# Earlier turns, smaller banks and moved counts in a fused attention and top-1 expert kernel

## Chip, core and metric

The kernel runs on one core of a Trainium2 chip. The metric is the device time of one execution in microseconds; before the change it is 443.85 us, the median of 3 runs (443.0 to 445.07). The profiled execution took 443.64 us, of which the profile shows a span of 439.6 us from the first to the last instruction.

## What is computed

Two blocks follow each other. The first is a cross attention between the rows `x` of a batch and 32 state rows for each head: the rows read from the states, and the states are rewritten from the rows. The second sends each of the 4352 rows that come out to one of eight experts, by the largest logit, and scales the expert's output by the softmax weight of that logit.

```python
# x: (8, 8, 512, 64)   state: (8, 8, 32, 64)
scores = scale * x @ state.T                 # (B, H, 512, 32)
a = softmax(scores);   xread = a @ state     # (B, H, 512, 64)
scores2 = scale * state @ x.T                # (B, H, 32, 512)
a2 = softmax(scores2); sread = a2 @ x        # (B, H, 32, 64)
rows = concatenate([xread, sread], axis=2)   # -> (8 * 544, 512) after heads are merged
logits = rows @ w_gate                       # (4352, 8)
e = argmax(logits); g = softmax(logits)[e]
out = g * (relu(rows @ w1[e]) @ w2[e])       # w1: (8, 512, 1024)  w2: (8, 1024, 512)
```

## The kernel before

The kernel guesses one expert for each batch (the most frequent one among its `x` rows) and computes all 512 `x` rows of the batch with that expert as dense products. Since `xread = a @ state`, it first forms `G = state @ w1[e]` (names `pG`, `G`), so that the up product is `a @ G` (`ph`, results `hT`). The down product is `hT @ w2[e]` (`py` for batches 0 and 1). For batches 2 to 7 both products are done by halves, with seven products of half-size blocks in place of eight, and sums between them (`pX`, `pD`, `pY`, `pZ`, `pW`). The 256 state rows are sorted by expert and computed in rounds of four groups of 32 rows (`pgh`, `pgy`). Rows that don't fit the guess are computed behind a branch at the end, which is skipped if there are none.

Every engine keeps the order of the program (all operations are recorded through one helper, so nearly all profile lines carry the line L48; the names of the tiles tell them apart). Attention of a batch is cut into steps, and a step is taken at each "slot" between the pieces of the dense products:

```python
def stages(b):
    xt, sx = new_xt(), new_sx()
    turn_x(b, xt, slice(0, 4))            # VectorE turns x in 32x32 blocks, four heads at a time
    turn_x(b, xt, slice(4, 8))
    turn_states(b, gp.tensor_copy)        # stT: VectorE, then a copy by GpSimd
    yield
    states_gates(b)                       # pg: states times gate matrix
    pc = new_pc()
    scores(b, xt, pc, 0)                  # pc: scores of half of the heads
    yield
    scores(b, xt, pc, 1)
    for i in range(4): turn_scores(pc, sx, i)
    less_max(sx, ALL, gp)
    nm = write_max(pc)                    # maximum, and its scaling, by VectorE
    yield
    soft[b] = (sx,) + write_weights(pc, nm)
    exponential(sx, ALL); over_sum(sx, ALL, gp)
    yield
    turn_read(b)                          # aT, and its store to at_dram
    yield
    turn_write(b)                         # pt
    yield
    write_rows(b)                         # pw, xs, four stores to srow, then fetch_batch(b + 3)
    exps, gates = logits_x(b)             # pl, lg, and the choice of each row's expert
    yield
    exps(); xsT = turn_rows(b)            # pxs
    yield
    choose(b); logits_s(b, xsT); gates()  # pr (counts), eb (the batch's expert), pls
```

Batches 0 and 1 have an order of their own, as the kernel has nothing else to do while they start. The first loads are the gate's matrix `wg4` and half of batch 0's states on ScalarE's queue, the other half and `x` on SyncE's. The expert of batch 0 is guessed from the sums of its states (`pss`, `prg`), so that its weights can be loaded at once:

```python
act.dma_start(out=wg4[:], in_=moe_w_gate...)
load_states(0, sp, act); load_x(0, sp)
...
def begin():
    keep_warm(3)                          # products whose result nobody reads ("idle")
    # pss: sums of the states; prg: their logits; most(0, pr): the expert of batch 0
    keep_warm(9)
    turn_states(0, act.copy)
    xt, sx = new_xt(), new_sx()
    turn_x(0, xt, slice(0, 4))
    # loads of w1, x and states of batch 1, wg, w2, batch 2
    turn_x(0, xt, slice(4, 8))
    for g in range(2): scores(0, xt, pc, g)
    turn_scores(pc, sx, 0); less_max(sx, one, dve); exponential(sx, one)
    states_w1(G, w1s[0], stG[:, 0], (0,)) # pG, and two copies 128x512 to G by ScalarE
    ...
    keep_warm(5)
    up(G, aT[0], hT, one, fs=near)        # ph
    ...
    def beside():                         # taken between the products of the last up()
        ...
        yield
        # pre
        scores(1, xt, pc, 1)
        exps, gates = logits_x(0)
        # scores of batch 1 turned, less_max, write_max; stages(2) begins: turns of batch 2
        yield
        exps(); gates(); count(0); turn_write(0)
        exponential(sx, ALL); soft[1] = (sx,) + write_weights(pc, nm)
        over_sum(sx, ALL, dve); turn_read(1)
        yield
    up(G, aT[0], hT, half, beside())
```

Products rotate through four PSUM banks of one pool (`bank`); `pc` has banks of its own. At the end of a batch by halves the last product and the last sum are:

```python
product(pD, lambda f: Sa[:, f], W(1, 1), start=False)   # pD: one bank, two halves of 256
store(yB, 1, 0)
add(yA, pD, yA, 0)                                      # two sums 128x256 on VectorE
(store if b < B - 1 else store_each)(yA, 0, 1)          # the last batch: ACT's and SP's queue
```

After that every engine reads the count of rows that are left, and branches.

Of the kernel before, what the change touches and what calls it, by code (L numbers as in the profile page):

```python
# [20 lines left out]
def kernel(  # L21
# [88 lines left out]
    wg4 = att.tile([128, NDC, E], FP32, name="wg4")  # L110
    act.dma_start(out=wg4[:], in_=moe_w_gate.rearrange("(p c) e -> p c e", c=NDC))
    load_states(0, sp, act)
# [89 lines left out]
    def turn_x(b, xt, h):  # L202
        dve.transpose(xt[:, h].rearrange("p h c u t -> p (h c u t)"),
                      x_nat[b][:, h].rearrange("p h c d -> p (h c d)"))
# [20 lines left out]
    def scores(b, xt, pc, g):  # L225

        for u in range(2):
            for q in range(4):
                for i in range(4):
                    pe.matmul(pc[ts(q, 32), i, ts(g, 128)], lhsT=stT[b][ts(i, 32), 2 * q + g, u ^ (i % 2), :],  # L230
                              rhs=xt[ts(i, 32), 2 * q + g, :, u, :],
                              start=(u == 0), stop=(u == 1), skip_group_check=True)
# [23 lines left out]
    def write_max(pc):  # L256
        nm = att.tile([128, 2], FP32, tag="nm", bufs=2, name="nm")
        dve.tensor_reduce(nm[:], pc[:, :, 0:256].rearrange("p i (g s) -> p g i s", g=2), AX.XY, ALU.max)
        dve.tensor_scalar(nm[:], nm[:], -SCALE, None, ALU.mult)
        return nm  # L260

    def write_weights(pc, nm):

        a2 = att.tile([128, 2, NC, 128], FP32, tag="a2", name="a2")
        s2 = att.tile([128, 2], FP32, tag="s2", bufs=2, name="s2")
        for g in range(2):
            act.activation(a2[:, g].rearrange("p c (i t) -> p i c t", i=4),
                           pc[:, :, ts(g, 128)].rearrange("p i (c t) -> p i c t", c=NC),
                           AF.Exp, bias=nm[:, g:g + 1], scale=SCALE, accum_out=s2[:, g:g + 1])
        return a2, s2  # L270
# [4 lines left out]
    def new_xt():  # L275
        return att.tile([128, H, NC, 2, 32], FP32, tag="xt", bufs=1, name="xt")
# [19 lines left out]
    def write_rows(b):  # L296

        _, _, s2, a2T = soft[b]
        pw = bank("pw")[:, 0:128].rearrange("p (g d) -> p g d", g=2)
        for g in range(2):  # L300
            for c in range(NC):
                for q in range(4):
                    pe.matmul(pw[ts(q, 32), g], lhsT=a2T[:, g, c, ts(q, 32)], rhs=x_nat[b][:, 2 * q + g, c, :],
                              start=(c == 0), stop=(c == NC - 1), skip_group_check=True)
        xs = rows_of[b] = att.tile([128, 2, D], FP32, tag="xs", bufs=2, name="xs")
        for g in range(2):
            act.activation(xs[:, g], pw[:, g], AF.Copy, scale=s2[:, g:g + 1])
        for q in range(4):
            sp.dma_start(out=srow[ts(b % 4, NS), b // 4, ts(q, 128)], in_=xs[ts(q, 32)].rearrange("p g d -> p (g d)"))
        fetch_batch(b + 3)  # L310
# [6 lines left out]
    def turn_read(b, i=ALL):  # L317
        if b not in aT:
            aT[b] = att.tile([128, 4, 2, 128], FP32, tag="aT", bufs=NE, name="aTe")[:]
        dve.transpose(aT[b][:, i].rearrange("p i g s -> p (i g s)"),  # L320
                      soft[b][0][:, i].rearrange("p i b n -> p (i b n)"))
        if i.stop == 4:
            sp.dma_start(out=at_dram[b], in_=aT[b].rearrange("p i g s -> p (i g s)"))
# [11 lines left out]
    def stages(b):  # L335

        xt, sx = new_xt(), new_sx()
        turn_x(b, xt, slice(0, 4))
        turn_x(b, xt, slice(4, 8))
# [27 lines left out]
        logits_s(b, xsT)  # L367
# [10 lines left out]
    def logits_s(b, xsT):  # L378

        pl = bank("pls")[ts(b % 4, 32), 0:E]  # L380
        for q in range(4):
            pe.matmul(pl, lhsT=xsT[:, q, :], rhs=wg[:, q, :], start=(q == 0), stop=(q == 3), skip_group_check=True)
        dve.tensor_copy(out=lgs[ts(b % 4, 32), b // 4], in_=pl)
# [47 lines left out]
    def begin():  # L431
# [14 lines left out]
        keep_warm(9)  # L446
        turn_states(0, act.copy)
        xt, sx = new_xt(), new_sx()
        turn_x(0, xt, slice(0, 4))
# [7 lines left out]
        turn_x(0, xt, slice(4, 8))  # L457
        pc = new_pc()
        for g in range(2):
            scores(0, xt, pc, g)  # L460
# [6 lines left out]
        states_w1(G, w1s[0], stG[:, 0], (0,))  # L467
# [23 lines left out]
        xt, sx = new_xt(), new_sx()  # L491
        turn_x(1, xt, slice(0, 4))
        turn_x(1, xt, slice(4, 8))
# [4 lines left out]
        def beside():  # L498
# [12 lines left out]
            exps, gates = logits_x(0)  # L511
# [5 lines left out]
            early.append(stages(2))  # L517
            next(early[0])
            yield
            exps()  # L520
            gates()
            count(0)
            turn_write(0)
            exponential(sx, ALL)
            soft[1] = (sx,) + write_weights(pc, nm)
            over_sum(sx, ALL, dve)
# [46 lines left out]
    def states_w1(G, w1t, st, halves=(0, 1), bank=bank):  # L573

        for k in halves:
# [5 lines left out]
            for g in range(2):  # L581
                act.copy(G[:, g, ts(k, 512)], pg[g][:])
# [138 lines left out]
    def down_by_halves(b, hT, w2t, insert, between):  # L721
# [23 lines left out]
        def product(to, a, w, start=True, stop=True):  # L745
            for c in range(2):
                for f in range(4):
                    pe.matmul(to[:, c], lhsT=a(f)[:, ts(c, 128)], rhs=w[:, f], start=(start and c == f == 0),
                              stop=(stop and f == 3), skip_group_check=True)
            n[0] += 1  # L750
# [16 lines left out]
        def store_each(y, i, k):  # L767
            for c, q in enumerate((act, sp)):
                no_dep(q.dma_start(out=rows[:, 2 * i + c, ts(k, 256)], in_=y[:, c]))

        def add(y, p, u, i):
            for c in range(2):
                dve.scalar_tensor_tensor(y[:, c], p[:, c], g[2 * i + c], u[:, c], ALU.mult, ALU.add)
# [3 lines left out]
        yA, yB = new_y(), new_y()  # L777
# [4 lines left out]
        pD = new_bank("pD")  # L782
# [30 lines left out]
        add(yA, pD, yA, 0)  # L813
        (store if b < B - 1 else store_each)(yA, 0, 1)
# [175 lines left out]
    def rounds(r0, r1):  # L990
# [11 lines left out]
        for r in range(r0, r1):  # L1002
# [16 lines left out]
            for f in range(0, NFC, 4):  # L1019
# [6 lines left out]
                if r + 1 < r1 or f + 4 < NFC:  # L1026
                    for _ in range(3):
                        yield
# [5 lines left out]
    def first():  # L1034

        write_rows(0)
        yield
# [9 lines left out]
        gates()  # L1047
        yield
# [4 lines left out]
        for b in range(2):  # L1053
            logits_s(b, xsT[b])
# [8 lines left out]
    def attention():  # L1063

        gens, slot = [first()], 0
        while gens:
            b = 2 + slot // 3
            old, new = gens[:], slot % 3 == 0 and b < B
            begun = slot < 6
            if begun:  # L1070
                advance(gens, old[:1])
            if new:
                gens.append(early.pop() if early else stages(b))
                if b > 2:
                    next(gens[-1])
# [12 lines left out]
    def batch(b):  # L1088
# [3 lines left out]
        def between(c):  # L1092
            nonlocal G
            if c == (1 if b else 2) and b + 1 < B:
                G = states_w1(new_G(), w1s[b + 1], stG[:, b + 1])
            yield
            if c == 1 and 0 < b < B - 2:
# [19 lines left out]
        else:  # L1117
            down_by_halves(b, hT, w2s[b], slots, between_products)
# [4 lines left out]
        elif b + 1 < B:  # L1123
            hT = up(G, aT[b + 1], new_hT(), insert=slots, at=(1, 3, 5, 7) if b + 1 < NE else (1, 3, 4, 5, 6, 7))
        if b == 0:
# [14 lines left out]
    for b in range(B):  # L1140
        batch(b)
# [9 lines left out]
    with tc.If(number(rest_i, B * S + NG) > 0, label="rest"):  # L1151
# [3 lines left out]
        with tc.If(number(left_i, B * S) > 0):  # L1155
# [65 lines left out]
            fix.release()  # L1221

# [32 lines left out]
```

## Time and profile before

| | |
|---|---|
| time | 443.85 us (443.0 to 445.07) |
| span in the profile | 439.6 us, TensorE clock granted 0.999 |
| matrix products | 427.4 us busy, 3933 instructions |
| VectorE, ScalarE, GpSimd | 225.3, 127.6 and 153.4 us busy |
| moved by DMA | 110.04 MB, mean 250 GB/s |
| instruction fetches (queue q8) | 32 packets, 0.52 MB |
| load of batch 3's `x`: issue on SyncE's queue | 53.16 us |
| last product `pD` | begins at 430.84 us, takes 3.72 us |

An fp32 product appears as two instructions of TensorE, and its weight load as two more. The busy time of TensorE (PE) is the time in which at least one product instruction is under way; the profiler models the end of a product, so busy does not mean at peak. In a table by stretches of the span, the difference between a stretch and the busy time in it is time in which TensorE had no product. A list of waits gives what ended such a pause: an engine and tile, a transfer, or "issue" where nothing that the profile shows was waited for. In the timeline a line has start, duration, engine, operation, tiles as out<-in, and in brackets the pause ahead of it.

### The profile page before, as it was taken

Reading aid. Unit: us, or ns where it says so; the run is one execution under the profiler, and the core shown is the slowest. Engines: PE = TensorE matmul, PEld = TensorE weight load, DVE = VectorE, ACT = ScalarE, POOL = GpSimd, SP = SyncE. Lnnn points to the kernel's source line nnn. Section 1 sums busy time; section 2 is a strip of 40 time slices with the busy share of each in tenths; the row PEclk is TensorE's granted clock in tenths of the full one; section 3 lists DMA queues with packets and bytes.
Section 4 is the critical chain, followed back from the end, with each engine's and each line's share of the span. In section 5 each row is a group of like instructions: output and inputs, shape, how many; then the busy total and the mean of one; then the engine's idle time right before and its main releaser. Section 6 shows DMA issues by size and latency. Waiting matters only on the chain.

```text
span 439.6 us, 10186 instructions
## 1 busy us (share of the span) xinstructions
PE 427.4 (97%) x3933; PEld 289.9 (66%) x3933; DVE 225.3 (51%) x482; ACT 127.6 (29%) x287; POOL 153.4 (35%) x143
## 2 busy tenths in 40 slices
PE   8899989999999999999999999999999999999995
PEld 7675544555555457786768677776867685768673
DVE  4757784787796657333505261523442370527151
ACT  1544233452353442212311241013240242025100
POOL 2010131322422431573327424534335253644231
PEclk9999999999999999999999999999999999999999
DMA  6990289655493454899999799789947998884211
GB/s 185 338 327 7 88 275 324 188 197 159 134 364 111 146 199 146 273 322 399 382 387 325 287 345 392 260 266 397 386 148 250 400 380 270 298 285 170 95 49 59
DMA packets 64513, 110.04 MB, mean 250 GB/s; under 512 B 12943, under 2 KB 22415, under 8 KB 64464
## 3 DMA queue, kind: packets, MB, share of 16 engines
q1 hardware_dynamic: 60240, 99.99, 65.9%
q0 software_dynamic: 2240, 7.08, 4.2%
q10 hardware_dynamic: 1984, 2.31, 1.5%
q8 instruction: 32, 0.52, 0.5%
q14 instruction: 17, 0.14, 0.1%
HBM read 94.15 MB, written 14.95 MB: 248 GB/s over the span
## 4 chain that ended last, share of the span: by engine, by line
PE 85%; DVE 9%; issue 1%; SPq 1%; DMA 1%; POOL 1%; ACT 1%; POOLq 0%; DVEq 0%
PE ph L48 22%; PE pD L48 10%; PE pX L48 10%; PE py L48 7%; PE pY L48 5%; PE pZ L48 5%; PE pgy L48 5%; PE pgh L48 5%; PE pW L48 5%; PE pG L48 3%; PE pc L48 3%; DVE sx L48 2%; DVE xt L48 2%; PE pt L48 1%; DVE sm L48 1%
## 5 line engine op out<-in xcount | busy, mean ns | idle before, releaser
L48 PE MATMUL py<-w2t,hT 128*128 128x512 f32 x128 | 59.0, 604 | 0.0
L48 DVE TENSOR_TENSOR hT<-ph,hT 128x512 f32<-128x512 f32 x50 | 34.6, 692 | 40.7 <-PE ph L48 40.7
L48 POOL TENSOR_TENSOR Ta<-w2t,Ta 128x1024 f32<-128x1024 f32 x12 | 30.6, 2547 | 46.6 <-PE pD L48 26.7
L48 PE MATMUL pX<-w2t,hT 128*128 128x256 f32 x192 | 43.7, 381 | 0.0
L48 PEld LDWEIGHTS pX<-w2t,hT 128*128 128x128 f32 x192 | 36.2, 190 | 6.4 <-issue 1.7
L48 PEld LDWEIGHTS py<-w2t,hT 128*128 128x128 f32 x128 | 23.0, 189 | 25.6 <-issue 24.9
L48 DVE SCALAR_TENSOR_TENSOR yh<-pY,gw,yh 128x256 f32<-128x256 f32 x24 | 10.0, 477 | 54.3 <-PE pY L48 47.8
L48 ACT ACTIVATE hT<-ph 128x512 f32<-128x512 f32 (+2 forms) x50 | 22.9, 462 | 42.1 <-PE ph L48 42.0
L48 PE MATMUL ph<-aTl,G 128*128 128x256 f32 (+1 forms) x112 | 33.8, 444 | 0.0
L48 PE MATMUL ph<-aTe,G 128*128 128x128 f32 (+2 forms) x128 | 30.4, 388 | 0.6 <-DVE aTe L48 0.4
L48 ACT ACTIVATE yh<-pX,gw 128x256 f32<-128x256 f32 x36 | 14.5, 474 | 53.7 <-PE pX L48 52.6
L48 POOL DMA_DIRECT2D out_dram<-yh x23 | 16.8, 732 | 33.5 <-DVE yh L48 16.8
L48 ACT ACTIVATE hT<-hT 128x512 f32<-128x512 f32 x30 | 18.9, 630 | 30.7 <-DVE hT L48 30.7
L48 POOL TENSOR_TENSOR sx<-sx,mx 128x1024 f32<-128x1024 f32 x6 | 11.5, 1914 | 46.5 <-DVE mx L48 46.5
L48 PEld LDWEIGHTS ph<-aTl,G 128*128 128x128 f32 x112 | 20.6, 190 | 9.6 <-issue 7.7
L48 PEld LDWEIGHTS ph<-aTe,G 128*128 128x128 f32 x128 | 18.8, 191 | 9.4 <-issue 6.7
L48 ACT COPY G<-pG 128x512 f32<-128x512 f32 x32 | 17.0, 591 | 23.7 <-PE pG L48 23.7
L48 POOL COPY stT<-stT 64x512 f32<-64x512 f32 x7 | 4.3, 608 | 51.6 <-DVE first_e L48 19.7
L48 PE MATMUL pY<-Ta,Sa 128*128 128x256 f32 x96 | 22.2, 384 | 0.0
L48 PE MATMUL pZ<-Tb,Sb 128*128 128x256 f32 x96 | 22.1, 383 | 0.0
L48 PEld LDWEIGHTS pY<-Ta,Sa 128*128 128x128 f32 x96 | 17.8, 190 | 6.4 <-issue 3.4
L48 POOL TENSOR_TENSOR Tb<-w2t 128x1024 f32<-128x1024 f32 x6 | 14.2, 2370 | 22.2 <-issue 22.2
(176 smaller groups left out, 743.3 us busy)
## 6 DMA issues: line engine op xcount, KB each, us to landing
s<-in_moe_w_dram SPq DMA_DIRECT2D x192, 256.0 KB, 6.0
w2t<-in_moe_w_dram SPq DMA_DIRECT2D x32, 512.0 KB, 6.0
w1t<-in_moe_w_dram SPq DMA_DIRECT2D x28, 512.0 KB, 6.4
x_nat<-in_x_dram SPq DMA_DIRECT2D x16, 512.0 KB, 5.9
out_dram<-yh POOLq DMA_DIRECT2D x23, 256.0 KB, 5.3
at_dram<-aTl SPq DMA_DIRECT2D x6, 512.0 KB
w1t<-in_moe_w_dram SPq DMA_DIRECT2D x2, 1024.0 KB
out_dram<-y ACTq DMA_DIRECT2D x8, 256.0 KB, 7.0
```

Source lines behind the costliest of these rows:

```text
L48: ins = getattr(self.engine, name)(*args, **kw)
```

## The change

The change moves and cuts small pieces of work around the dense products; it changes neither the number of dense products nor their shapes. Its parts:

- The first loads: the states of batch 0 ahead of the gate's matrix on ScalarE's queue. Six idle products in place of nine. `xt` is two tiles of four heads each; batch 0's scores are done for the first four heads, then for the others, so that the first may begin after the first turn. Its first `G` copies are four of 128x256.
- Odd batches get `xt` in other memory (the place of `Sa` and `Sb`, which are used only later), so that a turn need not wait until the scores of the batch before are done.
- The scaling of the write maximum by -1/8 moves from VectorE to ScalarE.
- Batch 0's logits and route move behind the last up products; its count moves to a later slot. The turns of batch 2 move behind them.
- `fetch_batch(3)` is issued ahead of the stores of batch 0's written rows, and the store of batch 1's read weights (`keep_read(1)`) after them. The turns of batch 3 are taken one slot earlier.
- The logits of the written rows of batches 0 and 1 share a bank and a copy.
- `G` of batch 1 is formed one place later among the slots.
- The last batch's `pD` has a bank for each half, its `yA` lies in memory of its own, the last sums stand in both arms of the branch, and each half is stored as soon as it is summed. The last round of state rows takes one slot less, so its last product stands one place earlier.

```diff
@@ first loads
+    load_states(0, sp, act)
     act.dma_start(out=wg4[:], in_=moe_w_gate.rearrange("(p c) e -> p c e", c=NDC))
-    load_states(0, sp, act)
     load_x(0, sp)
@@ write_max / write_weights
-        dve.tensor_scalar(nm[:], nm[:], -SCALE, None, ALU.mult)
+        act.activation(nm[:], nm[:], AF.Copy, scale=-SCALE)
@@ new_xt
-        return att.tile([128, H, NC, 2, 32], FP32, tag="xt", bufs=1, name="xt")
+        return [(att, ffn)[b % 2].tile([128, 4, NC, 2, 32], FP32,
+                tag=("xt0", "xt1", "Sa", "Sb")[2 * (b % 2) + k], name="xt") for k in range(2)]
@@ write_rows
+        if b == 0:
+            fetch_batch(3)
         for q in range(4):
             sp.dma_start(out=srow[ts(b % 4, NS), b // 4, ts(q, 128)], in_=xs[ts(q, 32)]...)
-        fetch_batch(b + 3)
+        if b:
+            fetch_batch(b + 3)
@@ turn_read
-        if i.stop == 4:
+        if i.stop == 4 and b != 1:
+            keep_read(b)
@@ begin
-        keep_warm(9)
+        keep_warm(6)
...
-        for g in range(2):
-            scores(0, xt, pc, g)
+        for qs in ((0, 1), (2, 3)):
+            for g in range(2):
+                scores(0, xt, pc, g, qs)
...
-        states_w1(G, w1s[0], stG[:, 0], (0,))
+        states_w1(G, w1s[0], stG[:, 0], (0,), cut=2)
@@ beside
             scores(1, xt, pc, 1)
-            exps, gates = logits_x(0)
...
-            early.append(stages(2))
-            next(early[0])
             yield
-            exps()
-            gates()
-            count(0)
+            exps, gates = logits_x(0)
             turn_write(0)
             exponential(sx, ALL)
             soft[1] = (sx,) + write_weights(pc, nm)
+            exps()
+            early.append(stages(2))
+            next(early[0])
+            gates()
             over_sum(sx, ALL, dve)
             turn_read(1)
@@ first (steps of batches 0 and 1 beside the first down product)
         write_rows(0)
+        keep_read(1)
...
         gates()
+        count(0)
@@ attention
+            if slot == 2:
+                early.append(stages(3))
+                next(early[0])
@@ between (slots of the down product)
-            if c == (1 if b else 2) and b + 1 < B:
+            if c == 1 and b:
                 G = states_w1(new_G(), w1s[b + 1], stG[:, b + 1])
             yield
+            if c == 2 and not b:
+                G = states_w1(new_G(), w1s[b + 1], stG[:, b + 1])
@@ down_by_halves
+            pD = [late["ps_t"].tile([128, 512], FP32, tag="t", bufs=2, name="pE")[:, 0:256] for _ in range(2)]  # b = 7
...
-        add(yA, pD, yA, 0)
-        (store if b < B - 1 else store_each)(yA, 0, 1)
+        def last():
+            for c in range(2):
+                add(yA, pD, yA, 0, (c,))
+                if b == B - 1:
+                    store_one(yA, 0, 1, c)
@@ rounds
-                    for _ in range(3):
+                    for _ in range(3 if r + 1 < NRS else 2):
@@ the end
-    with tc.If(number(rest_i, B * S + NG) > 0, label="rest"):
+    with tc.If(number(rest_i, B * S + NG) > 0, label="rest") as cmp:
+        last()
...
+    with cmp.Else():
+        last()
```

## The prediction, made before the changed kernel ran

> **What bounds the kernel now.** I read the page first, then the table by stretches, then TensorE's own waits, then the timeline of the two ends. The page says that TensorE is busy for nearly the whole span and that the chain that ended last lies on it:
>
> ```profile
> PE 427.4 (97%) x3933; PEld 289.9 (66%) x3933; DVE 225.3 (51%) x482; ACT 127.6 (29%) x287; POOL 153.4 (35%) x143
> ...
> PE 85%; DVE 9%; issue 1%; SPq 1%; DMA 1%; POOL 1%; ACT 1%; POOLq 0%; DVEq 0%
> ```
>
> Busy time alone would end the argument at "2.7% is left". Where that rest lies matters more. I cut the span where the work changes (start, first batch's rows, first down product, second up product, attention done, halves), and asked for busy time by stretch; the first number after the stretch is its length, then busy us of each engine with its instructions, then clock, DMA share, GB/s:
>
> ```profile
> 0.00:16.00 16.00, 12.96 (x201) 10.90 (x202) 9.71 (x30) 3.74 (x7) 2.73 (x18) 1.00 0.76 246
> 16.00:38.00 22.00, 20.33 (x297) 16.25 (x297) 12.52 (x31) 10.75 (x38) 1.20 (x3) 1.00 0.80 249
> 38.00:64.00 26.00, 24.51 (x371) 12.74 (x381) 22.77 (x45) 9.52 (x23) 4.00 (x6) 1.00 0.39 128
> 64.00:84.00 20.00, 19.07 (x338) 9.62 (x338) 12.17 (x24) 7.62 (x19) 5.32 (x6) 1.00 0.78 251
> 84.00:164.00 80.00, 79.94 (x1226) 42.87 (x1198) 57.27 (x139) 32.68 (x83) 25.42 (x20) 1.00 0.59 196
> 164.00:435.00 271.00, 270.56 (x1551) 197.48 (x1548) 110.38 (x217) 63.26 (x121) 114.77 (x90) 1.00 0.79 282
> 435.00:439.60 4.60, 0.00 (x0) 0.00 (x0) 0.48 (x2) 0.00 (x0) 0.00 (x0) 0.89 0.18 61
> ```
>
> TensorE's idle time is length less busy: 3.04, 1.67, 1.49, 0.93, 0.06, 0.44 and 4.60 us. So 351 us in the middle hold half a microsecond of idle time, and a change that leaves the products alone can only win before 84 us and after 435 us: about 7 us there and 4.6 us here at the very most. Who ended TensorE's waits after 20 us (us in total, times, longest):
>
> ```profile
> PE pl L48 <- issue: 1.0, 1, 1.0
> PE pg L48 <- DVE stT L48: 1.0, 1, 1.0
> PE pg L48 <- POOL stT L48: 0.9, 2, 0.5
> PE pl L48 <- ACT xs L48: 0.6, 1, 0.6
> ```
>
> **What the Trainium skill says.** "Perfetto Trace Analysis", section "Identifying the Most-Contended Engine", says that matmul busy time is no good measure of the distance to roofline, because pipelined matmuls look smaller; I use it only to find idle time, and the trace agrees in one place: the 128x256 products have a mean of 381 ns but 16 of them take 3.45 us on the chain, 216 ns each. "Runtime: NRT & Kernel Launch", section "Instruction fetch mechanics", says that instructions come in blocks of 16 KiB (256 instructions) by DMA; the page's queue q8 has 32 packets and 0.52 MB, which is 16 KB each. Its claim that this is mostly hidden holds here but for one wait (below). "DMA: Bandwidth & Descriptors", section "Queues, rings and completion order", says that each DMA engine takes turns between queues and consumes one queue's descriptors in order; that decides what the new order of the first loads costs. "TensorE: Matmul & The Clock Gate", section "What's actually happening", says that the clock is released by recent activity; here the 18 idle instructions (9 products) need 3.64 us, some 0.2 us each, while later ones are at 0.14 us (10 in 1.38).
>
> **The change part by part.** The products of the two big stages are the same in number and shape, so the 351 us stay.
>
> 1. The start. Today:
>
> ```profile
> 5.61 3.64 PE L48 MATMUL idle<-ident 128*128 128x128 f32 x18
> 7.23 2.32 DVE L48 STREAM_TRANSPOSE xt<-x_nat 128x1024 f32<-128x1024 f32 x2
> 9.18 2.20 PE L48 MATMUL pc<-xt,stT 32*32 32x128 f32 x128
> 11.41 0.45 DVE L48 STREAM_TRANSPOSE sx<-pc 128x256 f32<-128x256 f32 x1 [1.86 <-PE pc L48]
> ```
>
> The idle products end at 9.2 us although the first half of xt is there after half of 2.32 us, at 8.4. Six products end at about 8.4 (a third of 3.64 less), half of the scores (1.1 us) then run beside the second turn, which ends at 9.5, and the other half end at 10.6 where all end at 11.4 today. That is 0.7 us for VectorE's chain. TensorE does not get it all: its next product, ph at 15.21, follows pG (12.27, which waits 0.90 us for w1's transfer) and five more idle products that end at 14.8; so ph can move by 0.4 us at most. The four 128x256 copies in place of two of 128x512 let ph begin after the first quarter of G, which is needed for that. Against it stands the new order of loads on ACT's queue: the gate's matrix, issued at 0.84 us today, is now issued after two state loads, at about 1.75, and the second of those takes 4.7 us to land (to 6.45). In-order rings shared with x's rows put the gate's landing near 5.5 us, where prg starts at 5.33 today; expert 0's number and the transfer of w1 behind it would be 0.2 us late. Net **-0.2 us**, and this is the step I trust least (-0.5 to +0.8).
>
> 2. Scaling of the write maximum moves from VectorE (0.17 us, eight times) to ScalarE. Once, at 25.02 us, it stands ahead of the turn of batch 1 for which TensorE waits 0.4 us at 28 us: **-0.1**.
>
> 3. The logits of batch 0 move behind the last up product and the count of batch 0 to a later slot. TensorE's "pl <- issue" wait of 1.0 us ends at no semaphore: 13 of 16 pl instructions run at 33.2 us, 3 at 34.85. An instruction packet of the q8 kind ran in the window 32.4 to 34.9, so I take it for an instruction fetch that came late while 128 small score products used up a block within 1 us. The new order puts 1.9 us of up products before that place, and three idle products fewer shift it by 12 instructions. I give its loss 7 in 10: **-0.7**.
>
> 4. Batch 3's x and state. Today the load stands in SyncE's order behind the store of batch 1's read weights (which waits for VectorE until 50.1) and four small stores:
>
> ```profile
> 48.85 1.25 DVE aTe L48
> ...
> 53.16 0.53 SPq L48
> ...
> 55.89 4.25 DMA st<-in_state_dram
> ```
>
> Then VectorE turns it (61.09 to 62.9), GpSimd copies, and TensorE waits 1.00 and 0.47 us at 63 us. The change issues the load as soon as batch 0's x is free (pw ends at 42.6), stores batch 1's weights afterwards, turns batch 3 one slot earlier, and gives odd batches an xt of their own. The bus moved next to nothing from 33 to 44 us (7 GB/s in a slice), so x lands near 48 us and is turned by about 51, 10 us ahead: **-1.5**.
>
> 5. Batch 1's G moves one place back, behind pxs, pt and pc. Today pG, two pxs and waits for banks take 68.52 to 71.34, 2.82 us; pG alone takes 1.88 on the chain at 126.99 and two pxs some 0.2: **-0.7**. The wait of pl for xs at 79.18 (0.64) should go too, as ScalarE and VectorE are ahead: **-0.6**.
>
> 6. The end. Today both last sums wait for all 16 instructions of pD in one bank:
>
> ```profile
> 430.84 3.72 PE L48 MATMUL pD<-w2t,Sa 128*128 128x256 f32 x16
> 434.60 0.88 DVE L48 SCALAR_TENSOR_TENSOR yh<-pD,gw,yh 128x256 f32<-128x256 f32 x2 [2.73 <-PE pD L48]
> 435.50 0.35 SPq L48 DMA_DIRECT2D out_dram<-yh  x1
> ```
>
> With a bank for each half, the first sum and its store go 1.7 us earlier, and the second starts at 434.6 instead of behind the first: one sum of 0.48 us less, **-0.4**. Reading the branch's count ahead of the sums wins nothing more: SyncE's read and branch lie beside the landing of its own store. The earlier slot for the last round's product moves 3.6 us of work past other work, sum zero.
>
> Sum: 0.2 + 0.1 + 0.7 + 1.5 + 0.7 + 0.6 + 0.4 = 4.2 us, so 443.85 - 4.2 = 439.6 us, -0.9%.
>
> **Rivals.** (a) A wait takes the place of the one removed. VectorE is the fullest engine from 38 to 64 us (22.77 of 26), and batch 3's turn (2.34 + 0.66 us) now stands ahead of batch 1's route and batch 2's scores. For it: VectorE runs in order. Against it: sums and maxima of batch 1 begin some 3 us earlier, since lg no longer stands before them at 35.3 (idle for 7.2 us until then). If it bites, items 4 and 5 give back 2 us: 441.6. (b) The gate's matrix lands last of all first loads, near 6.5 us: then expert, stT and both turns are 1.1 us late, and item 1 becomes +0.8: 440.6. (c) Instruction fetches come late elsewhere, since every block's border is shifted; one costs about 1 us: 440.6; or the wait of item 3 stays: 440.3. (d) All hidden gains come in full and the start gives 0.5: 439.0. A DMA bound is unlikely: the share is 0.39 in the stretch where loads move.
>
> **Range and chances.** Two of the rivals at once give about 442; everything well and half a microsecond of luck gives 437.5, and the three runs of before lie 2 us apart. A gain of 2% is 8.9 us, more than the idle time before 84 us and after the last product can give together in any likely way; 2% slower would need a new wait of 9 us, and nothing that moves feeds the products after 164 us late. So: faster by over 2% 0.04, within 0.95, slower 0.01.
>
> **What would show it.** Step 1: sx near 10.7 us and ph near 15.0, w1 issued near 7.3. Step 3: no "issue" wait on pl. Step 4: x_nat issued near 42 us, no pg wait on stT after 40 us. Step 5: pG behind pc, no pl wait on xs. Step 6: one sum only after pD. Wrong if TensorE's idle time before 84 us does not fall from 7.1 to about 3.3 us, or if the stretch of the halves grows beyond 270.6 us of busy time.

## The result and the profile after

The changed kernel takes 438.75 us (median of 6 runs, 438.17 to 439.57), the kernel before 443.21 us beside it (6 runs, 442.96 to 445.07): a ratio of 0.9893, with a 95% interval of 0.9873 to 0.9913. The prediction was 439.6 us. The profiled execution has a span of 434.3 us, where that of before had 439.6.

The page's first line and the shares of the chain that ended last, in the kernel after:

```profile
PE 425.9 (98%) x3927; PEld 289.6 (67%) x3927; DVE 220.3 (51%) x473; ACT 129.0 (30%) x297; POOL 153.3 (35%) x143
...
PE 95%; DVE 2%; DMA 1%; ACT 0%; issue 0%; ACTq 0%; POOL 0%; DVEq 0%
```

TensorE's share of the chain grew from 85% to 95%, while its busy time fell by 1.5 us only: what left the chain is work of VectorE (9% to 2%) and about 1% each of SyncE, GpSimd, ScalarE and waits for instructions. The busy time by stretch of the kernel after, in the columns of the prediction's table (length, then TensorE's busy time first):

```profile
0.00:16.00 16.00, 12.18 (x188) 10.22 (x188) 8.77 (x28) 3.72 (x8) 2.71 (x18) 1.00 0.68 224
16.00:38.00 22.00, 21.42 (x300) 17.19 (x301) 14.78 (x29) 11.55 (x39) 1.19 (x3) 1.00 0.86 265
38.00:64.00 26.00, 26.00 (x427) 13.69 (x426) 20.96 (x49) 9.40 (x27) 5.79 (x8) 1.00 0.44 143
64.00:84.00 20.00, 19.88 (x313) 10.09 (x312) 12.66 (x23) 8.96 (x23) 5.41 (x6) 1.00 0.84 265
```

Idle time is 3.82, 0.58, 0 and 0.12 us: 4.5 us before 84 us, where before had 7.1 and the prediction asked for about 3.3; by this sign of its own it missed. Its other sign did not appear: from 164 to 435 us TensorE is busy for 266.45 us, below 270.6 (the span ends earlier). The three later stretches did what was asked, and more; the first did the opposite and now holds nearly all of the idle time. TensorE's waits, now over the whole span (total us, times, longest), name the reason:

```profile
PE idle L48 <- POOL ident masks.py:199: 1.5, 1, 1.5
PE prg L48 <- DMA wg<-in_moe_w_gate_dram: 1.0, 1, 1.0
PE pG L48 <- DMA w1t<-in_moe_w_dram: 1.0, 1, 1.0
PE ph L48 <- DVE aTe L48: 0.4, 1, 0.4
PE pg L48 <- POOL stT L48: 0.3, 1, 0.3
PE pss L48 <- DMA st<-in_state_dram: 0.2, 1, 0.2
```

The waits of pl on "issue", of pg on VectorE and of pl on xs are gone. The first line is the same in both kernels. The second is new: prg waits for the gate's matrix.

To see where the time went I took the start times of five products that both timelines have, and the time from each to the next. The spans are 439.62 and 434.26 us to the hundredth.

| from, to | before, us | after, us | change | predicted |
|---|---|---|---|---|
| start, first ph | 15.21 | 16.14 | +0.93 | -0.2 (step 1) |
| first ph, first py | 22.82 | 21.23 | -1.59 | -0.8 (steps 2, 3) |
| first py, py behind pc of batch 3 | 26.86 | 25.11 | -1.75 | -1.5 (step 4) |
| that py, first ph of batch 1 | 19.80 | 18.36 | -1.44 | -1.3 (step 5) |
| that ph, last product (pD, after: pE) | 346.15 | 345.99 | -0.16 | 0 |
| last product, end | 8.78 | 7.43 | -1.35 | -0.4 (step 6) |

They add up to -5.36 us. The medians differ by 4.46 us and the two profiled executions (443.64 and 438.42 us) by 5.22, so a total near the predicted 4.2 does not mean that the terms were right: one failed by 1.1 us one way, and others by up to 1 us the other way. That they partly cancel is luck.

### The profile page after: what moved, and what is told of

Its sections match the earlier page's. It is cut to its first block, busy times and chain, and to the rows that moved or that the text cites. A ratio compares the mean times of both kernels' runs of the same rounds, so it can differ in the third digit from the quotient of the medians.

```text
span 434.3 us, 10177 instructions
## 1 busy us (share of the span) xinstructions
PE 425.9 (98%) x3927; PEld 289.6 (67%) x3927; DVE 220.3 (51%) x473; ACT 129.0 (30%) x297; POOL 153.3 (35%) x143
## 4 chain that ended last, share of the span: by engine, by line
PE 95%; DVE 2%; DMA 1%; ACT 0%; issue 0%; ACTq 0%; POOL 0%; DVEq 0%
PE ph L48 23%; PE py L48 13%; PE pX L48 10%; PE pD L48 8%; PE pY L48 5%; PE pZ L48 5%; PE pgh L48 5%; PE pgy L48 5%; PE pW L48 5%; PE pc L48 4%; PE pG L48 3%; PE pw L48 2%; PE pt L48 2%; PE pE L48 2%; DMA wg<-in_moe_w_gate_dram 1%; PE pl L48 1%
## 5 line engine op out<-in xcount | busy, mean ns | idle before, releaser
L48 ACT COPY G<-pG 128x512 f32<-128x512 f32 (+1 forms) x34 | 17.1, 568 | 24.3 <-PE pG L48 24.3
L48 ACT COPY hT<-ph 128x512 f32<-128x512 f32 x10 | 5.9, 586 | 55.1 <-issue 43.1
```

The costliest lines, as they stand in the source:

```text
L48: ins = getattr(self.engine, name)(*args, **kw)
```

## The experiments

Ten kernels ran, one of them twice, in three groups. Each group had its own runs of the kernel before, with medians of 443.59, 444.35 and 444.60 us, so kernels of different groups are compared by their ratio to it. In the diffs a minus is the kernel that the experiment starts from.

### The gate's matrix first again

```diff
-    load_states(0, sp, act)
     act.dma_start(out=wg4[:], in_=moe_w_gate...)
+    load_states(0, sp, act)
     load_x(0, sp)
```

> The changed kernel with one line moved back: the gate's matrix is loaded ahead of batch 0's states again. Theory: in the changed kernel the gate's matrix landed last of ScalarE's loads (6.16 us), prg waited for it 0.96 us, and the pause kept TensorE's clock at half until 11.4 us, so that the scores took 2.88 us and ph began at 16.14 instead of 15.21. With the gate first: prg near 5.4 us, clock full from 8.5 us, sx near 10.7, ph near 14.9; 1.2 us less than the changed kernel, 437.5 us, ratio to the kernel before 0.987. Rival A: six idle products are too few, and the clock comes late whatever the order of loads: scores still 2.9 us, ph near 15.6, 438.2 us. Rival B: the later states cost as much as the earlier gate wins: no difference, 438.7 us.

Measured: 437.19 us (436.68 to 437.48), ratio 0.9861, interval 0.9845 to 0.9878. TensorE's timeline of the start (start us, us, instruction; in brackets the idle time before and what ended it), first of the kernel after, then of this one:

```profile
6.29 0.35 PE L48 MATMUL prg<-wg,sums 128*1 128x8 f32 x8 [0.96 <-DMA wg<-in_moe_w_gate_dram]
...
9.43 2.88 PE L48 MATMUL pc<-xt,stT 32*32 32x128 f32 x128
```

```profile
5.38 0.35 PE L48 MATMUL prg<-wg,sums 128*1 128x8 f32 x8 [0.26 <-DVE sums L48]
5.66 2.93 PE L48 MATMUL idle<-ident 128*128 128x128 f32 x12
8.52 2.19 PE L48 MATMUL pc<-xt,stT 32*32 32x128 f32 x128
12.34 1.21 PE L48 MATMUL pG<-w1t,stG 64*32 64x512 f32 x16 [1.63 <-DMA w1t<-in_moe_w_dram]
...
14.70 1.50 PE L48 MATMUL ph<-aTe,G 128*128 128x128 f32 x12
```

prg starts 0.91 us earlier, and the same 128 score instructions take 2.19 us instead of 2.88, as the clock is full at 8.9 us here and at 11.4 us there by the trace's clock record (last section). So the scores end 1.60 us earlier. Of this ph gets 1.44 us (16.14 to 14.70), for it no longer waits for aTe but follows pG, which waits 1.63 us for w1, and the idle products. So the order of the first loads costs the change 1.44 us in these two profiles, and all the rest of step 1 gains 15.21 - 14.70 = 0.51 us. The 1.44 is not a fixed size: in the six profiles whose start is that of the changed kernel, ph begins between 15.56 and 16.46 us, which is 0.86 to 1.76 us later than here. All runs of this version are faster than all of the changed kernel, though the intervals of the two ratios overlap slightly (0.9873 to 0.9878).

### Nine idle products with the gate first

```diff
-        keep_warm(6)
+        keep_warm(9)
```

> The change with the gate's matrix loaded first again (as in the run before, 437.2 us) and, besides, 9 idle products again instead of 6. Theory (the scores of batch 0 stand behind the idle products): pc starts at 9.1-9.2 instead of 8.52, sx at 11.2-11.4 instead of 10.75, first ph at 15.1-15.2 instead of 14.70; the time is 0.3 to 0.6 us above 437.2. The order of products by half heads alone, with 9 idle ones, is then worth nothing. Rival (pG waits for w1 anyway, so TensorE's chain does not see the idle products): first ph within 0.15 us of 14.70 and the same time.

Measured: 437.69 us (437.11 to 439.3), ratio 0.9863, interval 0.9821 to 0.9905. pc starts at 9.10 as the theory said, sx at 11.16, ph at 14.96 behind a wait of 0.27 us for aTe. So the three idle products are worth 0.26 us at ph, not 0.4 to 0.5, and what else the change does at the start (half heads, copies of G by quarters) the other 0.25 us of the 0.51, where I had expected nothing. The kernel before with six idle products, in the first of its profiles below, has ph at 14.96 as well, so each of the two parts is worth 0.25 to 0.26 us with or without the other. In the whole time the ratios are too alike to show 0.26 us.

### Two idle products fewer before the first ph

```diff
-        keep_warm(5)          # between pG and the first ph, gate first
+        keep_warm(3)
```

> The version with the gate's matrix first (437.2 us) with 3 instead of 5 idle products between pG and the first ph. There ph (14.70) follows the idle products without a wait, while its operands are ready at 14.40 (aTe written 13.95 + 0.45). Theory: ph starts at 14.40 to 14.50 and the time falls by 0.2 to 0.4 us, at most. Rival (the place in the instruction stream is worth more than that: 8 instructions fewer move every later block border): an issue wait of 0.3 to 1.0 us appears in one of the groups of short products (pc, pl, pw), and the time is the same or up to 0.7 us longer.

Measured: 437.67 us (436.74 to 437.94), ratio 0.9834, interval 0.9811 to 0.9857, which overlaps that of the gate first; no gain is shown. TensorE's timeline:

```profile
14.65 2.02 PE L48 MATMUL ph<-aTe,G 128*128 128x128 f32 x16 [0.36 <-DVE aTe L48]
```

VectorE wrote aTe at 14.05 + 0.45 us here, so ph was bound to it, and the theory's 0.2 to 0.4 us came to 0.05. No issue wait appeared either. With the gate first, the idle products behind pG and VectorE's chain end within 0.3 us of each other, so cutting one of them alone wins next to nothing.

### Batch 3 loaded and turned late

```diff
-        if b == 0:
-            fetch_batch(3)
         ...                                    # the four stores to srow
-        if b:
-            fetch_batch(b + 3)
+        fetch_batch(b + 3)
@@
-            if slot == 2:
-                early.append(stages(3)); next(early[0])
```

(and the store of batch 1's read weights ahead of it, as before)

> The changed kernel with batch 3's part undone: x and states of batch 3 are loaded behind the stores of batch 0's written rows and of batch 1's read weights, and batch 3 is turned at its old slot. Theory: the load is issued near 52 us, lands near 57.5, the turn ends near 62, and TensorE waits 1.2 to 1.6 us ahead of pg near 61.3 us: 440.1 us. Rival: VectorE, 3 us ahead since the logits of batch 0 moved, had already removed that wait: less than 0.4 us, 438.9 us.

Measured: 439.06 us (438.22 to 439.81), ratio 0.9895, interval 0.9878 to 0.9911: no difference in the whole time can be seen, so I read the place itself. From the start of pw to pc of batch 3 it is 2.97 us in before, 1.23 after and 2.30 here, between what the theory and the rival said: 1.07 us of step 4 come from the early load and turn, and the other 0.67 us come without them, which I put down to VectorE being ahead. From pc of batch 3 to the first ph of batch 1 it is 19.36 us here as in the kernel after, so nothing wins the 1.07 us back.

### Only the turn late

```diff
-            if slot == 2:
-                early.append(stages(3)); next(early[0])
```

> The change with one part undone: batch 3 is still loaded early, but turned at its old place, one slot later, and no longer ahead of slot 2. Theory (VectorE runs some 3 us ahead at that place, so the early turn is only a spare): the time and the first pc of batch 3 (61.48 in the changed kernel) agree within 0.3 us, the pg wait on stT is below 0.4 us. Rival (the early turn is what takes the two pg waits away): pg waits of 0.5 to 1.0 us come back at 61 us and the time grows by 0.5 to 1.0 us.

Measured: 439.40 us (438.77 to 440.3), ratio 0.9896, interval 0.9857 to 0.9936. The theory fell, in the timeline of TensorE:

```profile
61.01 0.23 PE L48 MATMUL pg<-wg,stT 64*32 64x8 f32 x2 [0.23 <-DVE stT L48]
61.77 0.27 PE L48 MATMUL pg<-wg,stT 64*32 64x8 f32 x14 [0.54 <-POOL stT L48]
```

Both waits are back although x had been issued at 41.47 us, and pw to pc is 2.30 us, as with the late load. So the early load alone moves nothing: VectorE reaches the turn at 58.00 us, and even the late load's x was in time for that (turned at 58.81, in a kernel whose first ph was 0.80 us later). The early turn is what gains the 1.07 us. It needs the early load so that it can stand where it stands, at 48.51 us: the late load is issued only at 51.98.

### One pair of xt buffers for all batches

```diff
-        return [(att, ffn)[b % 2].tile([...], tag=("xt0", "xt1", "Sa", "Sb")[2 * (b % 2) + k], ...
+        return [att.tile([...], tag=("xt0", "xt1")[k], bufs=1, ...
```

> The change with the same turned-x buffers for every batch, where the change gives odd batches buffers of their own. Theory: the turn of batch 3 at slot 2 then waits for the scores of batch 2 to have read the buffers, and as VectorE runs in order, the route of batches 0 and 1 and expert 1's number behind it come 5 to 6 us late (eb of batch 1 57.77 to about 63, issue of the second w1 58.52 to about 64), so the products of batch 1 wait for w1: 3 to 6 us slower than the change. Rival (the buffers are a spare, because the scores of batch 2 are done before VectorE comes to the turn): within 0.3 us of the change.

Measured: 442.04 us (440.92 to 442.9), ratio 0.9940, interval 0.9920 to 0.9960. That is 3.3 us more than after by the medians and 2.1 us by the ratios (0.47% of 443); the span is 438.4 us, 4.1 more. VectorE's turn of batch 3, and the two waits of TensorE that follow from it:

```profile
53.19 2.37 DVE L48 STREAM_TRANSPOSE xt<-x_nat 128x1024 f32<-128x1024 f32 x2 [4.28 <-PE pc L48]
```

```profile
PE pG L48 <- DMA w1t<-in_moe_w_dram: 1.8, 2, 1.2
...
PE pr L48 <- DVE oh L48: 0.9, 1, 0.9
```

The turn waits 4.28 us for the scores of batch 2 and holds up what stands behind it in VectorE's order: eb of batch 1 comes at 61.91 us (after: 57.77), w1 is issued at 62.58 (58.52), and pG is caught by it for 1.17 us. The theory had 5 to 6 us of delay; it was 4.1. The odd batches' own buffers are what makes the early turn possible.

### Batch 1's G at its old place

```diff
-            if c == 1 and b:
+            if c == (1 if b else 2) and b + 1 < B:
                 G = states_w1(new_G(), w1s[b + 1], stG[:, b + 1])
             yield
-            if c == 2 and not b:
-                G = ...
```

> The changed kernel with G of batch 1 formed at its old slot, ahead of pxs and pt. Theory: four banks filled by pG make pxs wait for ScalarE's first copies and pw's rows are late, so that pl waits for xs: 0.7 to 1.4 us more, 439.4 to 440.1 us, and the waits between pG and pt are back. Rival: the waits came from VectorE being late, which is no longer so: no difference, 438.7 us.

Measured: 440.27 us (439.75 to 440.57), ratio 0.9925, interval 0.9908 to 0.9941. The rival fell, and the theory holds in part. TensorE's timeline:

```profile
65.80 1.08 PE L48 MATMUL pG<-w1t,stG 64*32 64x512 f32 x12
67.88 1.91 PE L48 MATMUL pG<-w1t,stG 64*32 64x512 f32 x20 [1.00 <-DMA w1t<-in_moe_w_dram]
```

From the py before to the py behind, this stretch takes 10.48 us (62.17 to 72.65); it took 8.53 before and 7.94 after. So the move is worth 2.54 us in the changed kernel. Of this 2.04 is what the theory had not seen: with everything earlier the old place lies ahead of w1's landing, and from the start of pG to pxs it is 3.92 us (65.80 to 69.72) where pG takes 1.88 in both other kernels. The other 0.50 us is mostly the wait for banks that the theory named: from pxs to pt it is 0.86 us here and 0.22 in the kernel after. The wait of pl for xs did not come back, though: the next stretch to py is 5.49 us here, 5.48 after, 6.33 before. So it is not the place of G that removed it; that ScalarE and VectorE are ahead is the reason left, and no run tries it.

### The last sums ahead of the branch

```diff
-    with tc.If(number(rest_i, B * S + NG) > 0, label="rest") as cmp:
-        last()
+    last()
+    with tc.If(number(rest_i, B * S + NG) > 0, label="rest"):
         ...
-    with cmp.Else():
-        last()
```

> The changed kernel with the last sums and stores ahead of the branch again, banks still split. From the start of the last 128x256 product to the end of the span the kernel before has 8.8 us and the changed one 7.5. Theory: the split bank is worth 0.4 to 0.5 us of that, and the place behind the branch 0.8, since SyncE's branch and eight of its checks of semaphores then no longer stand behind the last store: this kernel has 8.3 us, and is 0.8 us slower than the changed one, 439.5 us. Rival: all of it comes from the split bank and the branch lies beside the store's landing, as the prediction has it: 7.5 us and no difference.

Measured: 439.31 us (439.0 to 439.92), ratio 0.9908, interval 0.9891 to 0.9924. From the start of the last product to the end it is 8.26 us here, 8.78 before and 7.43 after: the banks by halves gain 0.52 us, and the place in both arms of the branch 0.83. The end of the kernel after:

```profile
428.84 0.48 DVE L48 SCALAR_TENSOR_TENSOR aTl<-pE,gw,aTl 128x256 f32<-128x256 f32 x1 [0.93 <-PE pE L48]
430.49 0.48 DVE L48 SCALAR_TENSOR_TENSOR aTl<-pE,gw,aTl 128x256 f32<-128x256 f32 x1 [1.17 <-PE pE L48]
```

One sum follows the product, as predicted. For the 0.83 us the trace's records of SyncE give the reason. In the kernel before, it issues its store at 435.50 us, reads the count at 435.90 and branches at 436.41; the store lands at 437.39, and behind the landing stand 20 semaphore events (instructions by which an engine waits for others or signals to them) of the branch and of the end, so that the span ends 2.23 us after it. With the sums ahead of the branch it is the same: landing at 433.15, 20 events, 2.23 us. With the sums in both arms SyncE has branched at 409.09 us. Of its events 11 now lie between its store and the landing (432.87 us) and 8 behind it, and the end comes 1.39 us after the landing.

### Six idle products in the kernel before, three times

```diff
-        keep_warm(9)
+        keep_warm(6)      # first and third run; second run, also: keep_warm(5) -> keep_warm(8) before the first ph
```

> The kernel before with 6 idle products instead of 9 at the start (the change's cut alone), which puts every later TensorE instruction 12 places earlier in the instruction stream. Theory (the 1.0 us 'issue' wait behind the 13th of 16 pl instructions is an instruction fetch that came late): the block border now lies 12 places further on in the work, behind pl and some three products into ph, so no wait stands inside pl; a wait of 0 to 0.5 us is left in the ph products that follow, and the first py, less what the start itself moves, comes 0.5 to 1.0 us earlier (38.03 before). Rival (the wait belongs to pl itself, to its operands or its bank): a wait of 0.9 to 1.1 us stays behind the same 13th pl instruction. At the start, fewer idle products with the gate matrix first should bring the first ph from 15.21 to about 14.8-15.2 (scores of both heads halves still wait for the whole turn: sx no earlier than 11.3). Time under the theory: 0.5 to 1.2 us less than before; under the rival 0 to 0.3.

> The kernel before with 3 idle products moved from the first group (9 to 6) to the second (5 to 8): every later TensorE instruction keeps its place in the instruction stream of the kernel before. Theory (late instruction fetch at a block border): the wait is back inside pl, behind the 13th of its 16 instructions, with 0.9 to 1.1 us, where the run with 6 and 5 had it 0.44 us long inside ph; first ph at 15.2 and the time within 0.7 us of before. Rival (the start's earlier timing took the wait away, not the place of the border): no issue wait inside pl.

> A second profile of the kernel before with 6 idle products. Theory: the issue wait lies again inside ph behind its third product (0.3 to 0.6 us) and not inside pl, and the first py is at 37.1, as in the first; what followed the two pg waits there (the granted clock at 0.50 from 63.3 to 66.5 us, the next eight py 1.15 us longer) is chance, so that at even odds it is not seen again, and then batch 1's G comes 0.9 us earlier than in the kernel before (67.6 against 68.52). Rival: the low clock after the two waits is there again, at the same place.

Measured: 444.08 us (442.99 to 445.68), ratio 1.0001, interval 0.9984 to 1.0018; the second 444.53 us (442.65 to 445.9), ratio 0.9998, interval 0.9985 to 1.0011; the third 445.05 us in one run. In the first two no difference from before can be seen, against the 0.5 to 1.2 us of the theory. The issue wait, first in the kernel before, then in the first two of these timelines:

```profile
33.20 0.63 PE L48 MATMUL pl<-aTe,gst 128*32 128x128 f32 x13
34.85 0.41 PE L48 MATMUL pl<-aTe,gst 128*32 128x128 f32 x3 [1.02 <-issue]
```

```profile
34.88 1.35 PE L48 MATMUL ph<-aTe,G 128*128 128x256 f32 x5 [0.44 <-issue]
```

```profile
34.19 0.63 PE L48 MATMUL pl<-aTe,gst 128*32 128x128 f32 x13
35.12 0.41 PE L48 MATMUL pl<-aTe,gst 128*32 128x128 f32 x3 [0.30 <-issue]
```

Twelve instructions fewer (six products' and six weight loads') move it twelve instructions on, into ph: three of pl and three of ph, each with its weight load. Twelve put back elsewhere return it behind the 13th pl instruction. So the place is a place in the instruction stream. The size was wrong: 0.30 us instead of 0.9 to 1.1, as TensorE came to it 0.99 us later (pl at 34.19 instead of 33.20) and the block was ready at nearly the same time (35.12 instead of 34.85). In the third run there is no issue wait at all (pl at 34.17, then ph without a pause): TensorE came late enough. That part of its theory fell too. In the kernel after, pl runs at 35.86 us, 2.98 us after the start of the instruction packet (32.88), where the waits end 2.3 to 2.4 us after it (last section). So there, too, the work comes later than the block; no wait is merely shifted.

Why did the second and third come late, and why did the first not gain from its 0.95 us (first py at 37.08 instead of 38.03)? The second and third lost it at the start: ph begins at 16.19 and 16.18 us where the first has 14.96. The same 16 products of pG in the first and in the third:

```profile
12.26 1.21 PE L48 MATMUL pG<-w1t,stG 64*32 64x512 f32 x16 [1.14 <-DMA w1t<-in_moe_w_dram]
```

```profile
12.32 2.08 PE L48 MATMUL pG<-w1t,stG 64*32 64x512 f32 x16
```

The clock was not full there. The first lost it at 63 us, as its busy time by stretch shows (at the end of a line: granted clock, DMA share, GB/s):

```profile
62.00:64.00 2.00, 1.47 (x80) 1.19 (x80) 1.55 (x3) 0.23 (x2) 1.41 (x4) 0.79 0.93 360
64.00:66.00 2.00, 2.00 (x21) 0.84 (x3) 0.27 (x1) 0.00 (x0) 1.70 (x1) 0.50 0.97 342
```

After the two pg waits the clock stood at half for 3.41 us, and py to pG took 4.78 us instead of 3.63. In the second and third, with the same two waits, it did not fall, so this is chance, as the theory of the third said; but in the third G came at 68.10 us, not 67.6, and then waited 0.42 us for w1.

## Why the prediction was right, and where not

The total was right within 1 us, partly by luck, as steps 1 and 6 failed in opposite directions. The frame was right: the 346 us of the later products moved by 0.16 us, and everything else happened before 84 us and at the end. Step by step:

1. **The start: wrong, +0.93 instead of -0.2.** The failing step is the landing of the gate's matrix, "near 5.5 us". It was issued at 1.79 us and took 4.37 us, to 6.16, as the chain of the kernel after shows:

```profile
1.79 4.37 DMA wg<-in_moe_w_gate_dram
6.16 0.14 issue
6.29 0.35 PE prg L48 x8
```

Rival (b), which put the landing near 6.5 and the cost at +0.8, is what happened. All this was readable beforehand: the second state load, issued at almost the same time on the same queue, took 4.7 us to land in the kernel before, and the gate's matrix behind it should have been given no less than about 4.4. The "rings shared with x's rows" do not fit either, as x is on SyncE's queue. What the prediction did not count is the clock, which rises later behind the pause. The gain that it was to bring at ph was sized well: "at most" 0.4 us, measured 0.51 with the gate first. One sum in it is wrong, without harm: 9.2 less a third of 3.64 is 8.0 and not 8.4; with the gate first, the six products end at 8.6 us. That w1 would be issued near 7.3 us held only with the gate first (7.17); in the kernel after it was 8.07.
2. **Scaling moved to ScalarE: the size fits, the cause is not shown.** From the first ph to the first pc of batch 1 it is 13.76 us before and 13.57 after, 0.19 less, with the pg wait at 0.26 instead of 0.38 us. No run tells this part from others.
3. **The issue wait: right that it goes; mis-sized.** The 7-in-10 allowance gave 0.7; the wait and what it brings measured more. From the first pc of batch 1 to py it is 9.06 us before and 7.66 after, 1.40 less. Of this 1.02 is the wait itself; 0.23 is that the three pl instructions behind it took 0.34 us where three of 16 in 0.58 us take 0.11; 0.11 is batch 0's count, which is paid later (pr at 56.43 takes 0.21 us, before 0.10). That sum leaves 0.04. That the wait is an instruction fetch is borne out by the two moves of its place and by the packet ahead of each wait; that it went because the work comes later relative to the block, as the prediction's "1.9 us of up products before that place" had it, fits the third run of before with six idle products, in which TensorE came late and did not wait. "128 small score products used up a block within 1 us" misreads the timeline: a pc group there is 64 instructions and 64 weight loads, half a block.
4. **Batch 3: right, -1.75 instead of -1.5.** But the working put the load first and the turn last, and it is the reverse: without the early turn, 1.07 us come back whether the load is early or not; the other 0.67 us is probably VectorE's lead, which the prediction used only as an argument against rival (a). x was issued at 42.06 us and turned by 50.9, as said.
5. **G's place: right in sum (-1.44 against -1.3), with one reason missing.** The stretch with pG gained 0.59 us and the pl wait 0.85. The first is what "2.82 less 2.1" said. Here are pxs and pt in the kernel before, then in the one after:

```profile
70.40 0.78 PE L48 MATMUL pxs<-ident,xs 128*128 128x128 f32 x2
71.34 1.15 PE L48 MATMUL pt<-ident,a 128*128 128x128 f32 x8 [0.16 <-ACT G L48]
```

```profile
66.01 0.38 PE L48 MATMUL pxs<-ident,xs 128*128 128x128 f32 x2
66.23 1.38 PE L48 MATMUL pt<-ident,a 128*128 128x128 f32 x8
```

From one to the other it is 0.94 and 0.22 us; of these 0.72 us pt gives 0.23 back. What the prediction did not see is that in the changed kernel the old place would lie ahead of w1's landing and cost 2.04 us more. The gain at pl is not due to G's place, as the kernel with the old place keeps it.
6. **The end: mis-sized, -1.35 instead of -0.4.** The banks gave 0.52 where 0.4 was said. "Reading the branch's count ahead of the sums wins nothing more" is the sentence that failed: it won 0.83 us. Its reason is true as far as it goes: SyncE's read and branch, at 435.90 and 436.41 us, do lie beside the landing at 437.39. But 20 semaphore events follow that landing in the kernel before, and 8 in the changed one; these the prediction did not count.

Rival (a) did not happen: no wait of TensorE on VectorE is left between 20 and 84 us. Rival (c) did, once: in the kernel with the sums ahead of the branch, an issue wait of 0.32 us cuts the pc products, in TensorE's timeline:

```profile
68.47 0.44 PE L48 MATMUL pc<-xt,stT 32*32 32x128 f32 x13 [0.32 <-issue]
```

A shifted border alone does not explain it. The kernel after has the same TensorE instructions up to there and no wait, with its packet started at 65.69 us instead of 66.17 and this pc at 67.54 instead of 67.20.

Rival (d), 439.0, comes nearest to the measured 438.75, but not for its reasons: the start lost 0.93 us instead of winning 0.5, and the end won more than three times what was said.

## What to carry to other kernels

Read the landing times of the loads that are there before you reorder them, and give a load that moves behind another about the other's landing, not an average; here 16 KB at the wrong place cost 1.44 us where the rest of step 1 gained 0.51. When a change moves several waits at once, ask of each move what it protects in the new timing: the early turn is worth nothing without the odd batches' own buffers, and the late G, besides its own saving, keeps clear of a transfer that the old order would now run into. And at the end of a kernel count what an engine still has to do after its last store has landed: here a branch taken ahead of the last sums left 12 semaphore events fewer there, which was worth 0.83 us, more than the split of the banks.

## What the runs showed of the hardware

**The clock comes and goes in steps of 3.41 us.** "TensorE: Matmul & The Clock Gate" of the Trainium skill, section "What's actually happening", says that activity is judged in windows of about 3.4 us which run freely. The clock records agree: the stretch of full clock is 423.25, 426.67 or 430.08 us long in twelve of the thirteen profiles, each 3.41 or 3.42 apart, and in the other one 54.61 and 372.05 us, with 3.41 us of half clock between.

**In six profiles of one start, ph begins the later the later the clock rises.** The clock is full from 8.3 to 9.2 us in the kernel before, in the three changed kernels with the gate first, and in the first profile of before with six idle products. With the gate late, TensorE pauses 1 us ahead of prg, and the clock is full from 10.17, 10.50, 10.62, 11.41, 11.78 and 12.04 us in the six profiles; their ph begins in the same order, at 15.56, 15.79, 15.83, 16.14, 16.36 and 16.46. In the other two of before with six idle products, where pc pauses 0.45 us for xt near 9.2 us with the clock still low, it is full only from 13.8 and 15.2. The order by half heads lets the scores run on without that pause, and may be worth more by this than by the 0.25 us. But that such a pause is the cause is not shown: no run tried it by itself, and 15.16 us less two steps of 3.41 is 8.33, the moment at which the clock rose in the kernel with the gate first and nine idle products after nearly the same work. So one step was missed there ahead of the pause.

**The full clock was once lost without an idle window.** In the first profile of before with six idle products, TensorE ran 0.2 us of py, 1.1 of pw, some 0.4 of pg and the first 0.2 of pc in the 3.41 us up to 63.15, and the clock then fell to half. The same page says that it falls after at least one idle window; the measurement decides, and here TensorE was busy for 1.93 us of the window, with two pauses of 1.01 and 0.47 us. This is no rule, though: in the second profile the window from 61.57 to 64.98 us (steps of 3.41 counted on from the rise of its clock) holds the same two pauses and 1.94 us of busy time, and there the clock stayed. What tells the two apart is open. In the kernel before, the window from 59.70 to 63.11 us holds only the first of the pauses, and 2.41 us of busy time.

**An instruction block is ready about 2.35 us after its packet starts.** From the start of the 16 KB instruction packet to the end of the issue wait it is 2.39 us in the kernel before (32.46 to 34.85), and 2.35, 2.38 and 2.30 in the three other issue waits shown here (32.53, 32.74 and 66.17 to 34.88, 35.12 and 68.47); the packet itself takes 1.0 to 1.2 of it. All four waits stand in or just behind a group of pc, with 64 product instructions and 64 weight loads in 1.0 us, so such groups are where to look for fetches.
